# A fused attention and MLP kernel: quarters of M computed beside halves of the scores

## The chip, the cores and the metric

The kernel runs on one core of a Trainium2 chip. What counts is the device time of one execution in microseconds (us); of several runs the median is taken. TensorE (PE, with its weight loads as PEld) does the matrix products, VectorE (DVE) and ScalarE (ACT) read their results from the accumulation banks (PSUM) and do the rest, and SyncE (SP) issues all transfers (DMA).

## The reference

Eight batches of eight heads, 576 positions, head width 64. A packed set of 32 queries `p` attends to `k`, `v`; then every query attends to the 32 packed rows; the result goes through two feed-forward layers.

```python
def sm_attn(qq, kk, vv):
    s = scale * np.matmul(qq, kk.transpose(0, 1, 3, 2))
    a = np.exp(s - np.max(s, axis=-1, keepdims=True))
    return np.matmul(a / (np.sum(a, axis=-1, keepdims=True) + 1e-09), vv)
p_packed = sm_attn(p, k, v)
out = sm_attn(q, p_packed, p_packed)
x = out.transpose(0, 2, 1, 3).reshape(B * S, H * D)     # 4608 x 512
h = np.maximum(x @ w_in, 0.0); x = h * h @ w_out        # 512 -> 2048 -> 512
h = x @ w_in2; return (h / (1.0 + np.exp(-1.702 * h))) @ w_out2
```

## The kernel before

The program has two parts. The first, some 740 us long, does the attention and the first feed-forward layer, and prepares the weights of the second one beside it. The second part does the second layer; the change doesn't touch it.

**Slots.** The first layer runs in slots `(b, hf, fc)`: one batch, one half (288 positions), one of 16 chunks of 128 hidden units; from batch 2 on a batch is 32 slots in a row. Instead of `a @ v` and then `@ w_in`, the kernel multiplies the packed rows into the weights once for a batch: M = packed rows x `w_in`, made in four quarters `f` of 512 hidden units. A slot has a first product `h` (`mm1`, six matmuls of the attention `a` with M), the square of its positive part split into a high and a low number (`gh`; by `r`, `gf` and `gsplit`), and a second product `y` (`mm2`, twelve matmuls of `gh` with `w_out` into four banks `acc0` to `acc3`). The first product runs three slots ahead (`LA = 3`). At the end of a half (`fc` 15) the four banks are read out, by ACT (`ysb`) or, where a stored part is added, by DVE (`yp`), and slot `fc` 0 starts new sums in them.

**Attention beside it.** While batch b-1 goes through its 32 slots (from s0), the attention of batch b is spread over the same slots by a table: scores of the packed queries `s1` in two halves (slots 0 and 1), exponentials `s1b`, transposes `tr`, packed rows `pv` and `t2`, scores of all queries `s2a` in two halves (slots 12 and 17), `s2b`, `s2c`, and the quarters of M (`m_step`, slots 19, 21, 26, 29). In the traces both kinds of scores are called `s` and a quarter of M `m`. Each of them is one call of `heads`: eight small products that use a 64-row by 32-column part of the array each. They show as 16 matmuls, two rounds over the eight parts.

**Banks.** Of the eight banks, four are `acc`, two `mm` (used in turn by `h`) and two `at`: from batch 1 on all of the attention's products go to the `at` pair. A first half of `s1` is read twice: DVE takes the maxima (`L319`), then ACT copies it to `e` (`L323`). The second half stays in its banks until the exponentials. `s2a` is read by two DVE transposes (`L401`).

**Loads.** Tables also place the loads: `p` and all of `k` at slot -5, `v` at -2, `q` at 2, 3, 5, 6, and the eight halves of `w_in` (`win`, three buffers) at 9 and at the slots of the quarters of M.

The loop that sets the order:

```python
for s in range(done("y"), len(slots)):
    ...                              # gh of the slots up to s + 2
    drain(first, nfirst)             # h of slot s + 3
    drain(second, s)                 # y of slot s
    interleave(plan[s])              # the attention's steps of this slot
```

Of the kernel before, what the change touches and what calls it, by code (L numbers as in the profile page):

```python
# [75 lines left out]
def fused_kernel(ctx, tc, qT, kT, vv, pT, w_in, w_out, w_in2, w_out2, out):  # L76
# [216 lines left out]

    def att_tile(b, alt, name):

        pool, tag = (mm_p, "mm") if b == 0 and alt else (at_p, "at")
        return pool.tile([P, 512], F32, tag=tag, name=name)

    def heads(ps, w, x):

        n = None
        for hp in range(4):
            for r in range(2):
                rows = slice(64 * r, 64 * r + 64)
                xx = x(hp)[rows]
                n = xx.shape[-1]
                nc.tensor.matmul(ps[r][32 * hp:32 * hp + 32, :n], w(hp)[rows], xx, start=True, stop=True)  # L307

    def s1(b, hf):
        c = slice(hf * HS, (hf + 1) * HS)  # L310
        ps = [att_tile(b, hf, f"s1_{b}_{hf}_{r}") for r in range(2)]
        heads(ps, lambda hp: pt[b][:, hp, :], lambda hp: kt[b, hp][:, c])
        if hf == 0:
            rs[b] = st_p.tile([P, 6, 2], F32, tag="st", name=f"st{b}")
        st = rs[b]
        e1[b, "ps", hf] = ps
# [30 lines left out]
    def tr(b, r):  # L347
        e = e1.pop((b, r))
        if b == 0 and r == 1:
            t = y_p.tile([P, NDM * HS], F32, tag="y", name=f"e1t_{b}_{r}")[:, :5 * P]  # L350
        else:
            t = e1t_p.tile([P, 5 * P], F32, tag="e1t", name=f"e1t_{b}_{r}")
        t = e1T[b, r] = t.rearrange("p (c k) -> p c k", c=5)
        pa_ = att_tile(b, r, f"tr_{b}_{r}_a")
        pb_ = att_tile(b, r, f"tr_{b}_{r}_b")
        for c in range(4):
            nc.tensor.transpose(pa_[:, c * P:(c + 1) * P], e[:, c * P:(c + 1) * P], ident)  # L357
        nc.tensor.transpose(pb_[:64, :P], e[:, 512:576], ident)
        yield 1
        ta_ = t[:, 0:4, :].rearrange("p c k -> p (c k)")  # L360
        if b == 0:
            nc.vector.tensor_copy(ta_, pa_)
            yield 1
            nc.scalar.activation(t[:64, 4, :], pb_[:64, :P], AF.Copy)
        else:
            nc.scalar.activation(ta_, pa_, AF.Copy)
            yield 1
            nc.vector.tensor_copy(t[:64, 4, :], pb_[:64, :P])

    def pv(b, r):  # L370
        t = e1T.pop((b, r))
        v = vt.pop((b, r))
        ps = att_tile(b, r, f"pv_{b}_{r}")
# [69 lines left out]
    def s2c(b, hf):  # L443
# [3 lines left out]
        yield  # L447
        nc.vector.tensor_tensor(out=a[:, :, 1, :], in0=x, in1=a[:, :, 0, :].bitcast(F32), op=ALU.subtract)

    def m_step(b, f):  # L450
        w = [wt.pop((b, f, g)) for g in range(2)]
        if (b, f) == (0, 0):
            ps = [acc_p.tile([P, 512], F32, tag=f"acc{r}", name=f"m_{b}_{f}_{r}") for r in range(2)]
        else:
            ps = [at_p.tile([P, 512], F32, tag="at", name=f"m_{b}_{f}_{r}") for r in range(2)]
        heads(ps, lambda hp: ppT[b][:, 32 * hp:32 * hp + 32], lambda hp: w[hp // 2][:, hp % 2, :])
        yield 1
# [314 lines left out]
    def at(s, f, *a):  # L772
        plan[s].append((f, a))
# [83 lines left out]
    def token(k):  # L857
# [2 lines left out]
        g = running[k] if k in running and name != "warm" else macros[name](*map(int, a))  # L860
        running[k] = None if g is None or next(g, running) is running else g

    for b in range(1, B):
        if b == 1:
            s0 = 0
            at(43, m_step, 1, 2)
            at(47, m_step, 1, 3)
            for n, s in enumerate((40, 40, 43, 43)):
                at(s, load_win, 1, 2 + n // 2, n % 2)
            continue  # L870
        else:
            s0 = (b - 1) * 2 * NFC
            at_k, at_v, at_q, at_w = -5, -2, (2, 3, 5, 6), 9
            steps = [(0, s1, 0), (1, s1, 1), (4, s1b), (7, tr, 0), (8, pv, 0), (8, tr, 1), (9, pv, 1),
                     (10, t2), (12, s2a, 0), (16, s2b, 0), (17, s2c, 0), (17, s2a, 1), (20, s2b, 1), (26, s2c, 1)]

            steps += [(s, m_step, f) for f, s in enumerate((19, 21, 26, 29))]
        ld = loads(b)
        for n, (f, *a) in enumerate(ld):
            at(s0 + (at_k if n < 5 else at_v if n < 7 else at_q[n - 7]), f, *a)  # L880
        if b > 1:
            for s, f, *a in steps:
                at(s0 + s, f, b, *a)
        ws = [s for s, f, *_ in steps if f is m_step]
        if b == 2:
            at_w = 14
        for n in range(8):
            f = n // 2
            at(s0 + (at_w if n < 3 else ws[(n - 3) // 2]), load_win, b, f, n % 2)

# [106 lines left out]
    nfirst, nsplit = done("f"), done("g")  # L997
    for _ in range(4):
        ahead()
    for s in range(done("y"), len(slots)):  # L1000
        while nsplit < min(s + LA, nfirst):
            drain(parts, nsplit)
            nsplit += 1
        while nfirst < min(s + LA + 1, len(slots)):
            drain(first, nfirst)
            nfirst += 1
        while nsplit <= s:
            drain(parts, nsplit)
            nsplit += 1
        drain(second, s)  # L1010
        interleave(plan[s])
# [31 lines left out]
```

## Time and profile before

| | |
|---|---|
| three timed runs | median 1437.19 us, 1436.12 to 1437.35 |
| the profiled execution | 1436.79 us |
| its span, first to last instruction | 1434.9 us |
| PE busy, share of the span | 98% |
| PEld / DVE / ACT | 88% / 66% / 58% |
| granted TensorE clock, mean | 0.999 of full speed |

The profiled execution lies 0.4 us below the median. A busy PE isn't PE at its peak: matmuls overlap, so what a step costs is read from the start of one group to the start of the next.

### The profile page before, as it was taken

What the parts mean: (1) busy time and instruction counts of PE and PEld (TensorE: products, weight loads), DVE (VectorE), ACT (ScalarE), POOL (GpSimd) and SP (SyncE); (2) the same over time, 40 slices, a digit from 0 to 9 for tenths busy, and PEclk for the clock granted to TensorE, in tenths of its full rate; (3) what the DMA queues carried; (4) which work ended last, traced back from release to release, by engine and by line L of the source; (5) the groups of instructions that cost most, each with busy time, mean ns of one, the idle gap of its engine ahead of it and who ended that gap; (6) DMA issues with size and microseconds to landing.
All of it is one profiled execution on the core that took longest, in us unless ns stands there. A gap on an engine that the chain in (4) does not pass through costs nothing.

```text
span 1434.9 us, 24896 instructions
## 1 busy us (share of the span) xinstructions
PE 1412.7 (98%) x9734; PEld 1262.1 (88%) x9734; DVE 951.2 (66%) x1623; ACT 835.8 (58%) x1740; POOL 0.7 (0%) x6
## 2 busy tenths in 40 slices
PE   6999999999999999999999999999999999999999
PEld 4688989889898998999998888888888888999998
DVE  6896475756757657573255778577855875677585
ACT  5878676676776677765564544454444534544452
POOL 0000000000000000000000000000000000000000
PEclk9999999999999999999999999999999999999999
DMA  9848467576664756541325566656665676688675
GB/s 327 288 148 307 162 207 227 176 235 212 200 229 176 251 182 221 186 149 33 125 99 206 205 244 221 217 206 227 227 227 205 220 250 229 248 300 286 253 293 180
DMA packets 110934, 307.95 MB, mean 215 GB/s; under 512 B 9056, under 2 KB 52192, under 8 KB 96736
## 3 DMA queue, kind: packets, MB, share of 16 engines
q1 hardware_dynamic: 110816, 306.35, 62.1%
q8 instruction: 77, 1.26, 0.4%
q14 instruction: 41, 0.34, 0.1%
HBM read 250.94 MB, written 55.38 MB: 213 GB/s over the span
## 4 chain that ended last, share of the span: by engine, by line
PE 93%; DMA 3%; ACT 3%; DVE 1%; issue 0%; SPq 0%; DVEq 0%; ACTq 0%
PE h L112 37%; PE y L524 27%; PE o L112 24%; PE m L307 2%; PE s L307 1%; PE pv L377 1%; DMA wA<-w_d 1%; PE tr_a L357 1%; DMA win<-win_d 0%; DMA raw_wo<-in_w_out 0%; PE h L486 0%; DMA w_d<-wc 0%; DMA p<-in_pT 0%; PE warm L830 0%; ACT e L338 0%; ACT gh L202 0%
## 5 line engine op out<-in xcount | busy, mean ns | idle before, releaser
L524 PE MATMUL y<-gh,wo 128*128 128x288 f32 x2976 | 434.2, 295 | 0.4 <-ACT gh L202 0.2
L524 PEld LDWEIGHTS y<-gh,wo 128*128 128x128 f32 x2976 | 406.2, 188 | 4.4 <-ACT gh L202 1.3
L112 PE MATMUL h<-y,wA 128*128 128x512 f32 (+1 forms) x1680 | 349.8, 367 | 1.4 <-DMA wA<-w_d 1.4
L112 PE MATMUL o<-g,wB 128*128 128x512 f32 (+1 forms) x1680 | 349.0, 367 | 0.0
L112 PEld LDWEIGHTS h<-y,wA 128*128 128x128 f32 x1680 | 305.6, 188 | 42.1 <-issue 2.0
L112 PEld LDWEIGHTS o<-g,wB 128*128 128x128 f32 x1680 | 305.6, 188 | 39.6 <-DMA wB<-w_d 0.4
L112 PE MATMUL h<-a,M 128*128 128x288 f32 x1488 | 242.8, 299 | 1.3 <-ACT r L493 1.3
L112 PEld LDWEIGHTS h<-a,M 128*128 128x128 f32 x1488 | 207.7, 188 | 37.0 <-issue 27.7
L636 ACT ACTIVATE g<-hid 128x1024 fp32r<-128x1024 f32 (+1 forms) x140 | 132.8, 971 | 131.9 <-DVE hid L631 102.3
L204 DVE TENSOR_TENSOR gh<-gf,gh 128x288 fp32r<-128x288 f32 x248 | 111.6, 452 | 121.4 <-ACT gh L202 121.1
L612 DVE TENSOR_TENSOR g<-hid,g 128x1024 fp32r<-128x1024 f32 (+1 forms) x140 | 152.6, 1113 | 42.3 <-ACT g L636 40.7
L493 ACT ACTIVATE r<-h 128x288 f32<-128x288 f32 x256 | 104.1, 407 | 84.2 <-PE h L112 81.0
L700 ACT ACTIVATE r<-h 128x512 f32<-128x512 f32 (+1 forms) x120 | 66.6, 555 | 118.3 <-PE h L112 116.1
L708 DVE TENSOR_TENSOR hid<-h,r 128x512 f32<-128x512 f32 (+1 forms) x120 | 76.0, 634 | 81.7 <-PE h L112 65.3
L202 ACT ACTIVATE gh<-gf 128x288 fp32r<-128x288 f32 x248 | 108.6, 438 | 5.2 <-DVE gf L501 2.7
L718 DVE TENSOR_TENSOR hid<-hid,sg 128x512 f32<-128x512 f32 (+1 forms) x120 | 75.7, 631 | 47.1 <-ACT sg L714 47.0
L503 ACT ACTIVATE gf<-r 128x288 f32<-128x288 f32 x212 | 94.3, 445 | 6.6
L714 ACT ACTIVATE sg<-hid 128x512 f32<-128x512 f32 (+1 forms) x120 | 70.2, 585 | 30.5 <-DVE hid L708 30.3
L470 DVE TENSOR_TENSOR M<-m,M 128x512 fp32r<-128x512 f32 x62 | 41.9, 688 | 45.9 <-ACT M L468 45.2
L631 DVE TENSOR_TENSOR hid<-hid 128x1024 f32<-128x1024 f32 (+1 forms) x60 | 66.1, 1111 | 0.0
L468 ACT ACTIVATE M<-m 128x512 fp32r<-128x512 f32 x62 | 36.0, 593 | 39.8 <-PE m L307 39.7
L714 ACT ACTIVATE sg<-h 128x512 f32<-128x512 f32 (+1 forms) x40 | 22.3, 557 | 32.7 <-PE h L112 32.7
(110 smaller groups left out, 974.5 us busy)
## 6 DMA issues: line engine op xcount, KB each, us to landing
wB<-w_d SPq DMA_DIRECT2D x70, 1024.0 KB, 5.0
wA<-w_d SPq DMA_DIRECT2D x40, 1024.0 KB, 4.9
wA<-w_d SPq DMA_DIRECT2D x40, 768.0 KB, 6.2
win<-win_d SPq DMA_DIRECT2D x56, 512.0 KB, 5.1
w_d<-wc SPq DMA_DIRECT2D x112, 256.0 KB, 3.4
k<-in_kT SPq DMA_DIRECT2D x32, 288.0 KB, 5.4
y_d<-ysb SPq DMA_DIRECT2D x16, 576.0 KB, 3.8
v<-in_vv SPq DMA_DIRECT2D x16, 512.0 KB, 7.0
```

Of the source, the lines that this page charges most:

```text
L112: nc.tensor.matmul(ps, w, x, start=start and i == 0, stop=stop and i == n - 1, skip_group_check=more)
L202: nc.scalar.activation(hi, x, AF.Copy)
L204: nc.vector.tensor_tensor(out=lo, in0=x, in1=hi.bitcast(F32), op=ALU.subtract)
L493: nc.scalar.activation(r, ps[:, :HS], AF.Relu)
L503: nc.scalar.activation(g, r, AF.Square)
L524: nc.tensor.matmul(accs[d][:, :HS], w[:, d * P:(d + 1) * P], t[:, x_, :], start=first, stop=fc == seg[1] and d not in {o[0] for o in ops[n ...
L612: nc.vector.tensor_tensor(out=t[:, :, 1, :n], in0=src, in1=t[:, :, 0, :n].bitcast(F32), op=ALU.subtract)
L636: nc.scalar.activation(t[:, :, 0, :PAIRS[p]], gop[p, i, g, "src"], AF.Copy)
L700: nc.scalar.activation(t[:, 0, :n], bank[p, c, "1"][:, :n], AF.Copy)
L708: nc.vector.tensor_tensor(out=hid(p, c, blk), in0=bank[p, c, b][:, :n], in1=part[p, c, r][:, 0, :n], op=ALU.add)
L714: nc.scalar.activation(t, bank[p, c, "1"][:, :n] if blk == 2 else hid(p, c, blk), AF.Sigmoid, scale=GELU)
L718: nc.vector.tensor_tensor(out=hid(p, c, blk), in0=bank[p, c, "1"][:, :n] if blk == 2 else hid(p, c, blk), in1=part.pop((p, c, "sg", blk)), ...
```

## The change

From batch 3 on, each half of `s1` is issued together with a quarter of M of the batch before (quarters 2 and 3, at slots 0 and 4), and from batch 2 on each half of `s2a` with a quarter of its own batch (0 and 1, now at slots 17 and 22). The scores of such a pair go to the two `mm` banks, the quarter to the two `at` banks. In such a slot the order is: `y` of the slot, scores, quarter of M, the reading of the scores, and only then `h` of slot s + 3. The slot behind it issues its `y` ahead of its own `h`. Both halves of `s1` are now copied to `e`. Quarters 2 and 3 of the last batch stay alone.

```diff
 def att_tile(b, alt, name):
-    pool, tag = (mm_p, "mm") if b == 0 and alt else (at_p, "at")
+    pool, tag = (mm_p, "mm") if alt else (at_p, "at")
...
 def s1(b, hf):
-    ps = [att_tile(b, hf, f"s1_{b}_{hf}_{r}") for r in range(2)]
+    ps = [att_tile(b, b > 2 or b == 0 and hf, f"s1_{b}_{hf}_{r}") for r in range(2)]
...
-            if b > 0 and hf == 0:
+            if b > 2 or b > 0 and hf == 0:
...
 def s2a(b, hf):
-    ps = [att_tile(b, hf == 0, f"s2_{b}_{hf}_{r}") for r in range(2)]
+    ps = [att_tile(b, b > 1 or b == 0 and hf == 0, f"s2_{b}_{hf}_{r}") for r in range(2)]
...
+            slot_p, slot_k, slot_v, slot_q, slot_w = -11, (-11, -8, -6, -4), (-16, -14), (2, 5, 7, 9), (10, 12, 14)
...
+            joint[s0] = (s1, b, 0), (m_mm, b - 1, 2)
+            joint[s0 + 4] = (s1, b, 1), (m_mm, b - 1, 3)
+            at(s0 + 1, m_ev, b - 1, 2)
+            at(s0 + 5, m_ev, b - 1, 3)
+        joint[s0 + 17] = (s2a, b, 0), (m_mm, b, 0)
+        joint[s0 + 22] = (s2a, b, 1), (m_mm, b, 1)
...
+        slot_w += (18, 20, 23, 25, 33)
...
+        if s in joint:
+            lead_split(s, min(s + LA, nfirst))
+            drain(second, s)
+            (f, *a), (f2, *a2) = joint[s]
+            g = f(*a)
+            next(g)
+            drain(f2, *a2)
+            for _ in range(4 if f is s1 else 2):
+                next(g)
+            lead(s)
+            interleave([(lambda g=g: g, ())] + plan[s])
+        else:
+            if s - 1 not in joint:
+                lead(s)
+            drain(second, s)
+            lead(s)
+            interleave(plan[s])
```

`m_mm` is the matmul part of `m_step` and `m_ev` its reading, now apart; `lead(s)` issues `h` of slot s + 3 and `gh` of slot s.

The first place is PE at the change from batch 2 to batch 3 (slot 96, where the scores of batch 4 are due). `y_1_*` are the second products of the half that ends, `y_0_*` of the half that begins, `h_0_3` is a first product. Before:

```order
L524 MATMUL y_1_2_0_3695<-gh_1_15_4192,wo_1843 128x288
L524 MATMUL y_1_3_0_3698<-gh_1_15_4192,wo_1843 128x288
L112 MATMUL h_0_3_4306<-a_0_3738,M_0_3834 128x288 x6
L524 MATMUL y_0_0_0_4317<-gh_0_0_4237,wo_514 128x288 x2
L524 MATMUL y_0_1_0_4320<-gh_0_0_4237,wo_514 128x288 x2
L524 MATMUL y_0_2_0_4323<-gh_0_0_4237,wo_514 128x288 x2
L524 MATMUL y_0_3_0_4326<-gh_0_0_4237,wo_514 128x288 x2
```

After the change, at the same place:

```order
L538 MATMUL y_1_2_0_3681<-gh_1_15_4183,wo_1843 128x288
L538 MATMUL y_1_3_0_3684<-gh_1_15_4183,wo_1843 128x288
L538 MATMUL y_0_0_0_4276<-gh_0_0_4213,wo_514 128x288 x2
L538 MATMUL y_0_1_0_4279<-gh_0_0_4213,wo_514 128x288 x2
L538 MATMUL y_0_2_0_4282<-gh_0_0_4213,wo_514 128x288 x2
L538 MATMUL y_0_3_0_4285<-gh_0_0_4213,wo_514 128x288 x2
```

`h_0_3` no longer stands between the last matmuls of one half and the first of the next, which write the same four banks.

The second place is PE a little further on, behind these second products. `s_4_0_*` are the scores of batch 4 (two tiles), `m_2_*` is quarter 2 of M of batch 3, `h_0_3` and `h_0_4` are first products. Before:

```order
L307 MATMUL s_4_0_0_4333<-k_3_4156,p_4148 32x288
L307 MATMUL s_4_0_1_4334<-k_3_4156,p_4148 32x288
L112 MATMUL h_0_4_4353<-a_0_3738,M_1_3920 128x288 x6
L524 MATMUL y_0_0_0_4317<-gh_0_1_4271,wo_514 128x288 x2
L524 MATMUL y_0_1_0_4320<-gh_0_1_4271,wo_514 128x288 x2
```

After the change:

```order
L307 MATMUL s_4_0_0_4292<-k_3_4177,p_3894 32x288
L307 MATMUL s_4_0_1_4293<-k_3_4177,p_3894 32x288
L307 MATMUL m_2_0_4303<-win_2_0_3860,ppT_3558 32x512
L307 MATMUL m_2_1_4304<-win_2_0_3860,ppT_3558 32x512
L307 MATMUL m_2_0_4303<-win_2_0_3860,ppT_3558 32x512
L307 MATMUL m_2_1_4304<-win_2_0_3860,ppT_3558 32x512
L307 MATMUL m_2_0_4303<-win_2_1_3994,ppT_3558 32x512
L307 MATMUL m_2_1_4304<-win_2_1_3994,ppT_3558 32x512
L307 MATMUL m_2_0_4303<-win_2_1_3994,ppT_3558 32x512
L307 MATMUL m_2_1_4304<-win_2_1_3994,ppT_3558 32x512
L112 MATMUL h_0_3_4319<-a_0_3892,M_0_3783 128x288 x6
L538 MATMUL y_0_0_0_4276<-gh_0_1_4241,wo_514 128x288 x2
```

The eight products of the quarter of M follow the scores, and the next first product, `h_0_3`, comes behind both.

The third place is ACT in the same slot. `ysb` is the last of the four readings of `acc`, `e_4_0` and `e_4_1` are the copies of the scores, `r` the positive part of a first product. Before:

```order
L538 ACTIVATE ysb_1_4297<-y_1_3_0_3698 128x288
L202 ACTIVATE gh_0_2_4303<-gf_0_2_4283 128x288
L493 ACTIVATE r_0_3_4313<-h_0_3_4306 128x288
L323 ACTIVATE e_4_0_4345<-s_4_0_0_4333 128x288
L323 ACTIVATE e_4_1_4348<-s_4_0_1_4334 128x288
L202 ACTIVATE gh_0_3_4350<-gf_0_3_4315 128x288
```

After the change:

```order
L552 ACTIVATE ysb_1_4267<-y_1_3_0_3684 128x288
L202 ACTIVATE gh_0_2_4273<-gf_0_2_4253 128x288
L325 ACTIVATE e_4_0_4314<-s_4_0_0_4292 128x288
L325 ACTIVATE e_4_1_4317<-s_4_0_1_4293 128x288
L507 ACTIVATE r_0_3_4326<-h_0_3_4319 128x288
L202 ACTIVATE gh_0_3_4342<-gf_0_3_4328 128x288
```

The copies now stand ahead of `r_0_3`, since `h_0_3` now comes behind the scores.

## Rows read from the trace of the kernel before

**Rows 1.** The page's chain of work that ended last, by engine

```profile
PE 93%; DMA 3%; ACT 3%; DVE 1%; issue 0%; SPq 0%; DVEq 0%; ACTq 0%
```

**Rows 2.** Busy time by stretch, each one batch long: stretch, length, engines, clock, DMA

```profile
227.36:317.10 89.74, 88.44 (x797) 80.26 (x796) 57.17 (x131) 61.32 (x158) 0.00 (x0) 1.00 0.66 204
317.10:404.62 87.52, 87.52 (x797) 80.10 (x796) 58.96 (x137) 62.67 (x159) 0.00 (x0) 1.00 0.65 212
404.62:492.43 87.81, 87.81 (x797) 80.28 (x796) 58.84 (x134) 62.21 (x160) 0.00 (x0) 1.00 0.60 198
```

**Rows 3.** Timeline of PE, 270 to 345 us: start, length, line, instruction, count

```profile
308.76 1.09 PE L307 MATMUL m<-win,ppT 64*32 64x512 f32 x16
309.78 1.06 PE L112 MATMUL h<-a,M 128*128 128x288 f32 x6
...
313.05 1.75 PE L524 MATMUL y<-gh,wo 128*128 128x288 f32 x12
314.64 0.95 PE L112 MATMUL h<-a,M 128*128 128x288 f32 x6
315.42 1.74 PE L524 MATMUL y<-gh,wo 128*128 128x288 f32 x12
317.10 0.72 PE L307 MATMUL s<-k,p 64*32 64x288 f32 x16
317.74 1.06 PE L112 MATMUL h<-a,M 128*128 128x288 f32 x6
318.64 1.74 PE L524 MATMUL y<-gh,wo 128*128 128x288 f32 x12
```

**Rows 4.** Timeline of PE, instants in batch 0's two score groups

```profile
19.15 0.48 PE L307 MATMUL s<-q,ppT 64*32 64x288 f32 x8 [0.30 <-ACT ppT L389]
...
19.41 0.65 PE L307 MATMUL s<-q,ppT 64*32 64x288 f32 x9
...
19.66 0.44 PE L307 MATMUL s<-q,ppT 64*32 64x288 f32 x6
```

**Rows 5.** Timeline of all engines, 312.8 to 319.5 us

```profile
312.71 0.69 DVE L470 TENSOR_TENSOR M<-m,M 128x512 fp32r<-128x512 f32 x1 [1.44 <-ACT M L468]
...
314.46 1.30 ACT L538 ACTIVATE ysb<-y 128x288 f32<-128x288 f32 x4
...
317.93 0.82 DVE L319 TENSOR_REDUCE st<-s 128x1 f32<-128x288 f32 x2 [0.97 <-PE s L307]
318.42 0.78 ACT L323 ACTIVATE e<-s 128x288 f32<-128x288 f32 x2 [2.02 <-DVE st L319]
```

**Rows 6.** Line 323: durations in ns, least, median, most

```profile
L323 ACT ACTIVATE e<-s x14: 392/412/446, 46.2 to 581.6; 128x288 f32<-128x288 f32 x14
```

**Rows 7.** Timeline of all engines, 132.5 to 137.5 us

```profile
133.70 1.29 DVE L470 TENSOR_TENSOR M<-m,M 128x512 fp32r<-128x512 f32 x2 [2.11 <-ACT M L468]
134.45 0.13 PEld L307 LDWEIGHTS s<-k,p 64*32 64x32 f32 x2 [1.02 <-DVE M L470]
```

**Rows 8.** Timeline of all engines, 437.9 to 439.3 us

```profile
438.00 0.72 PE L307 MATMUL s<-q,ppT 64*32 64x288 f32 x16
...
438.84 0.48 DVE L401 STREAM_TRANSPOSE s2t<-s 128x288 f32<-128x288 f32 x1 [1.53 <-PE s L307]
```

**Rows 9.** Timeline of all engines, 222.5 to 229.5 us

```profile
224.77 1.54 DVE L536 TENSOR_TENSOR yp<-y,yp 128x288 f32<-128x288 f32 x4
...
227.36 0.72 PE L307 MATMUL s<-k,p 64*32 64x288 f32 x16
```

**Rows 10.** Timeline of PE, 100 to 112 us

```profile
108.85 1.77 PE L112 MATMUL h<-a,M 128*128 128x288 f32 x12
```

**Rows 11.** Timeline of PE, 283 to 289 us

```profile
285.01 1.06 PE L307 MATMUL m<-win,ppT 64*32 64x512 f32 x8
287.38 1.06 PE L307 MATMUL m<-win,ppT 64*32 64x512 f32 x8 [1.30 <-DMA win<-win_d]
```

**Rows 12.** The tile win: time of its transfers from issue to landing

```profile
DMA to landing us min/median/max: 2.9/5.5/8.7
```

More of the change, by code (lines that the diff above doesn't have):

```diff
@@ L319, in s1 @@
             nc.vector.tensor_reduce(out=st[:, hf, r:r + 1], in_=ps[r][:, :HS], axis=AX.X, op=ALU.max)
-            if b > 0 and hf == 0:
+            if b > 2 or b > 0 and hf == 0:
                 yield 1
-                e = e1[b, r] = e1_p.tile([P, S], F32, tag="e1", name=f"e1_{b}_{r}")
-                nc.scalar.activation(e[:, :HS], ps[r][:, :HS], AF.Copy)
+                if hf == 0:
+                    e1[b, r] = e1_p.tile([P, S], F32, tag="e1", name=f"e1_{b}_{r}")
+                e = e1[b, r][:, c]
+                nc.scalar.activation(e, ps[r][:, :HS], AF.Copy)
                 e1[b, "ps", hf][r] = e
@@ L353, in tr @@
         t = e1T[b, r] = t.rearrange("p (c k) -> p c k", c=5)
-        pa_ = att_tile(b, r, f"tr_{b}_{r}_a")
-        pb_ = att_tile(b, r, f"tr_{b}_{r}_b")
+        pa_ = att_tile(b, b == 0 and r, f"tr_{b}_{r}_a")
+        pb_ = att_tile(b, b == 0 and r, f"tr_{b}_{r}_b")
         for c in range(4):
@@ L372, in pv @@
         v = vt.pop((b, r))
-        ps = att_tile(b, r, f"pv_{b}_{r}")
+        ps = att_tile(b, b == 0 and r, f"pv_{b}_{r}")
         for c in range(5):
@@ L448, in s2c, with m_mm @@
         nc.vector.tensor_tensor(out=a[:, :, 1, :], in0=x, in1=a[:, :, 0, :].bitcast(F32), op=ALU.subtract)
+    mps = {}
     def m_step(b, f):
+        yield from m_mm(b, f)
+        yield 1
+        yield from m_ev(b, f)
+    def m_mm(b, f):
         w = [wt.pop((b, f, g)) for g in range(2)]
@@ L455, in m_step, with m_ev @@
             ps = [at_p.tile([P, 512], F32, tag="at", name=f"m_{b}_{f}_{r}") for r in range(2)]
+        mps[b, f] = ps
         heads(ps, lambda hp: ppT[b][:, 32 * hp:32 * hp + 32], lambda hp: w[hp // 2][:, hp % 2, :])
-        yield 1
+        return
+        yield
+    def m_ev(b, f):
+        ps = mps.pop((b, f))
         if b == 0 and 4 * f < NFULL:
@@ L861, in token @@
         running[k] = None if g is None or next(g, running) is running else g
+    joint = {}
     for b in range(1, B):
         if b == 1:
-            s0 = 0
             at(43, m_step, 1, 2)
@@ L870, in fused_kernel @@
             continue
-        else:
[L872 to L889, printed above, removed]
+        s0 = (b - 1) * 2 * NFC
+        if b == 2:
+            slot_p, slot_k, slot_v, slot_q, slot_w = -5, (-5, -5, -5, -5), (-2, -2), (2, 3, 5, 6), (14, 14, 14)
+            steps = [(0, s1, 0), (1, s1, 1), (4, s1b), (7, tr, 0), (8, pv, 0), (8, tr, 1), (9, pv, 1), (10, t2)]
+        else:
+            slot_p, slot_k, slot_v, slot_q, slot_w = -11, (-11, -8, -6, -4), (-16, -14), (2, 5, 7, 9), (10, 12, 14)
+            steps = [(6, s1b), (9, tr, 0), (10, pv, 0), (10, tr, 1), (11, pv, 1), (12, t2)]
+            joint[s0] = (s1, b, 0), (m_mm, b - 1, 2)
[4 more added lines that the diff above has]
+        joint[s0 + 22] = (s2a, b, 1), (m_mm, b, 1)
+        steps += [(18, m_ev, 0), (19, s2b, 0), (21, s2c, 0), (23, m_ev, 1), (25, s2b, 1), (27, s2c, 1)]
+        slot_w += (18, 20, 23, 25, 33)
+        if b == B - 1:
+            steps += [(26, m_step, 2), (29, m_step, 3)]
+            slot_w = slot_w[:-1] + (27,)
+        for t, f, *a in ((slot_p, load_p), *((slot_k[i], load_k, i) for i in range(4)), *((slot_v[i], load_v, i) for i in range(2)),
+                         *((slot_q[i], load_q, i) for i in range(4)), *steps,
+                         *((t, load_win, n // 2, n % 2) for n, t in enumerate(slot_w))):
+            at(s0 + t, f, b, *a)
     calm = [s for s in range(45, SB - 2 * NFC) if s % 16 in CALM]
@@ L999, in fused_kernel, with lead_split, lead @@
         ahead()
-    for s in range(done("y"), len(slots)):
-        while nsplit < min(s + LA, nfirst):
+    def lead_split(s, end):
+        nonlocal nsplit
+        while nsplit < end:
             drain(parts, nsplit)
             nsplit += 1
+    def lead(s):
+        nonlocal nfirst
+        lead_split(s, min(s + LA, nfirst))
         while nfirst < min(s + LA + 1, len(slots)):
@@ L1006, in fused_kernel @@
             nfirst += 1
[L1007 to L1011, printed above, removed]
+        lead_split(s, s + 1)
+    for s in range(done("y"), len(slots)):
+        if s in joint:
+            lead_split(s, min(s + LA, nfirst))
+            drain(second, s)
[13 more added lines that the diff above has]
+            interleave(plan[s])
         for _ in range(plan_end[s]):
```

## The prediction

> **What bounds the kernel now.** I read the chain of work that ended last first: 93% of it is PE [rows 1], so only time that PE loses or gains counts. Then the busy time by stretch, one batch each. In the second stretch PE is busy from end to end (87.52 of 87.52 us) at a granted clock of 1.00; the stretches around it are 2.2 and 0.3 us longer with the same matmuls [rows 2]. So in this part PE waits for nearly nothing, and a step costs what it adds to PE's own row of groups. That is read from the timeline of PE, start to start [rows 3]. A plain slot is 1.59 us of `y` and 0.78 of `h`, 2.37 in all (313.05 to 314.64 to 315.42). A group of scores in between costs more than its own 0.64 us (317.10 to 317.74): the `y` ahead of it takes 1.68 instead of 1.59, the `h` behind it 0.90 instead of 0.78. So 0.09 on the way in, 0.12 on the way out. A quarter of M takes 1.02 us (308.76 to 309.78) and pays the same way in and out.
>
> **What a pair saves on PE.** The first saving is one way in and one way out: 0.21 us. The second is inside the groups. No pair of scores and M stands side by side before, but batch 0 has two groups of scores in a row [rows 4]: their first three rounds start at 19.15, 19.41 and 19.66, so the second group starts 0.25 us behind the last round of the first, as if it were the same group. A lone group takes 0.64, so 0.14 of it is a tail behind its second round, paid only where another kind of matmul follows. M's rounds are then (1.02 - 0.14)/2 = 0.44 us. A pair is 2 x 0.25 + 2 x 0.44 + 0.14 = 1.52 us in place of 0.64 + 1.02 = 1.66: 0.14 saved, 0.35 with the way in and out. Bounds for the inner part: nothing, if M has to wait for the tail of the scores, and 0.14; I take 0.14, since rows 4 are the same kind of neighbours.
>
> The row shows a price for each change between whole-array and 64-by-32 matmuls. The Trainium skill's page "TensorEngine Tiling (Array Packing)", Tiling Modes, Key Properties, says that changing the tiling mode drains TensorE, and changing only the tile does not; by that rule too a pair drains once instead of twice, and rows 3 and 4 agree. It gives no duration.
>
> There are 22 pairs: ten with `s1` (batches 3 to 7), twelve with `s2a` (batches 2 to 7). On the matmuls alone that is 22 x 0.35 = 7.7 us. Now what the new order adds.
>
> **The scores must be out of their banks before the next first product.** Before, scores lay in the `at` pair and `h` in the `mm` pair; `h` never waited for them. Now the scores take both `mm` banks, and `h` of slot s + 3 needs the first back at once. Count from the start T of the scores. With `s2a` the first DVE transpose starts 0.84 after T (438.84, scores at 438.00) and takes 0.48 [rows 8]; with 0.06 from an end to the waiting weight load (DVE's first reading of M ends at 133.70 + 0.69 = 134.39, the load starts at 134.45 [rows 5, 7]) the bank is back at T + 1.38, ahead of the end of M at T + 1.52. M hides it; 0.14 us is left over. With `s1` the bank is read twice, one after the other: maxima from T + 0.83 (317.93), and the copy, released by them, from T + 1.32 (318.42) [rows 5], for 0.41 [rows 6]. The bank is back at T + 1.79, and `h` starts 0.27 late. So an `s1` pair saves 0.08, an `s2a` pair 0.35: 10 x 0.08 + 12 x 0.35 = 5.0 us. Bounds for the 0.27: nothing, if copy and maxima could run together, and 0.27 more for each 0.27 by which DVE comes late; DVE sat idle for 0.97 before these maxima [rows 5], so I take 0.27.
>
> **At slot 0 of a batch `y` loses its cover.** In the first `s1` pair of a batch, `y` of `fc` 0 directly follows `y` of `fc` 15, and writes the four `acc` banks that ACT is only now reading out. Before, an `h` of 0.78 lay in between. ACT's four readings end at 314.46 + 1.30 = 315.76 [rows 5]. What comes behind the last reading is seen at the start of batch 2's slots, where `y` does wait: the readings, there by DVE, end at 224.77 + 1.54 = 226.31, and the next group starts at 227.36 [rows 9], 1.05 later. So here the scores would start at 315.76 + 1.05 = 316.81; without a wait at 314.64 + 1.68 = 316.32. That is 0.49 lost, in four of the five batches. In batch 3's case (the one of rows 9) the readings already bound the end, so moving `h` behind them loses its whole 0.78. Sum 4 x 0.5 + 0.8 = 2.8 us. Bounds: nothing, if ACT comes earlier for having one positive part less, and 5 x 0.78 = 3.9; I take 2.8, since the readings start when the last matmuls end, which the change does not move.
>
> **Loads.** The stretch that is 2.2 us longer has a quarter of M that stood between its two halves: 285.01 to 287.38, for `win` [rows 11]. That half was loaded two slots (4.7 us) ahead of its use, and such a transfer takes 5.5 us in the median and 8.7 at most [rows 12]. Now it is issued at slot 18 for slot 22, four slots or 9.5 us ahead, and the last half of a batch at slot 33 for 36. So I count the 2.2 and 0.3 us [rows 2] as gained: 2.5. Only in the last batch is a half still loaded two slots ahead (27 for 29); the six such loads of before cost 2.5 together, so 0.4 for this one. Bounds: gain of nothing, if other transfers come in its way, and 2.5. The loads of `k` and `v` are only moved to where SP has slots to spare; `k` still has four slots.
>
> **Small things.** Of two `h` in a row the second costs 1.77 - 0.95 = 0.82 us instead of 0.78 to 0.79 [rows 3, 10]: 22 x 0.03 = 0.7 us lost. The ten added copies are 4 us of ACT, which is busy for 62 of 88 us [rows 2]: hidden, unless they stand ahead of the positive part that the next slots wait for. `h` of slot s + 3 is now issued 1.6 us nearer to its `y`, with some 5 us left; between them lie four operations on ACT and DVE of the size of those in rows 6 and 8, 0.4 to 0.5 us each, about 2 in all.
>
> **Sum.** 5.0 + 2.5 - 2.8 - 0.4 - 0.7 = 3.6 us. The profiled execution took 1436.8, so 1433.2; it lies 0.4 below the median, so for a median 1433.6. About 0.2%, or 2.9 us, is what a measurement of this kernel can tell from no change; the line lies at 1434.3.
>
> **Rivals.**
> Readings that come late (the other side). The matmuls of a pair get shorter, the readings don't. If DVE has one more operation of 0.69 us [rows 5] in hand when the scores end, each `s1` pair loses 0.69 and each `s2a` pair 0.69 - 0.14 = 0.55: 10 x 0.69 + 12 x 0.55 = 13.5 us, and the time is 1447. It decides from a mean lateness of 0.24 us on, where the 3.6 are gone (10 x 0.24 + 12 x 0.10), and means slower by 0.2% from 0.37. For it: DVE and ACT are busy for two thirds of these stretches. Against it: DVE was idle for 0.97 and 1.53 us before the readings at 317.93 and 438.84 [rows 5, 8], and a new slot has two `y`, 3.2 us without a first product, for it to catch up. Chance 0.13, nearly all of it slower. The Trainium skill's tiling page (Performance Considerations, PSUM Bottleneck) warns of this: tiling speeds up TensorE, not the evacuation of PSUM, which may become the bottleneck. For `s1` the trace already bears it out, by the 0.27.
>
> The wait for `win` moves instead of going: the gain shrinks to 3.6 - 2.5 = 1.1, time 1435.7 for the execution, 1436.1 for a median. For it: transfers of up to 8.7 us, and loads now spread among the stores. Against it: three to four slots of lead. Chance 0.12.
>
> No saving inside a pair: M waits for the tail of the scores. For `s2a` pairs 0.14 less, for `s1` pairs nothing less until M ends at T + 1.66, still ahead of 1.79: 12 x 0.14 = 1.7 less, time 1435.3. Together with a wait at each slot 0 at its upper bound (1.1 more) 1436.4. Chance 0.09.
>
> Readings that don't hold: `h` waits for the maxima alone, or the `acc` banks are read out early enough: 2.7 or 2.8 more, time 1430.9. Against the first speaks that ACT's copy began with the end of the maxima each time. Chance 0.08.
>
> **How the numbers follow.** The forecast, 1433.6, has a chance of 0.58, with a range of its own from 1431.5 to 1435.5 by its bounds; 0.42 of that lies below 1434.3. Faster: 0.42 + 0.08 = 0.50. Same: 0.16 + 0.12 + 0.09 + 0.02 = 0.39. Slower: 0.11. The range from 1430.0 to 1437.0 takes in all but the late readings and the far end of the last rival.
>
> **What would show it.** In the changed profile: a pair from the start of the scores to the next `h` of 1.5 us with `s2a` and 1.8 with `s1`; at slot 0 a `y` of about 2.1 us ahead of the scores; no PE wait for `win` but perhaps in batch 7; stretches of a batch of about 87.3 us (87.5 less two times 0.35 and 0.08, plus 0.5 and four times 0.03). The prediction is wrong if `s2a` pairs take more than 1.6 us, if `y` waits for `gh` in the slots behind a pair, or if transfers hold PE elsewhere.

## The result and the profile after

The changed kernel takes 1443.94 us in the median of six runs (1443.05 to 1448.71), the kernel before 1437.27 in six runs on the same chip: the ratio is 1.0053, with a 95% interval from 1.0035 to 1.0070. It is slower by half a per cent, 6.7 us, where 3.6 us of gain were forecast, and it lies outside the range. The profiled execution of the changed kernel took 1446.28 us, span 1444.5, 2.3 above its median; its granted clock is 0.999 on the mean, as before.

First the busy time by stretch, one batch of slots each, the view that answers to [rows 2]: the stretch, its length, busy time of PE, PEld, DVE, ACT and POOL, granted clock, DMA share, GB/s. Then before's fourth stretch, which [rows 2] doesn't hold. The third fence has the page's chain of work by engine and answers to [rows 1].

```profile
222.60:317.12 94.52, 87.99 (x796) 80.97 (x795) 57.35 (x131) 61.40 (x160) 0.00 (x0) 1.00 0.60 193
317.12:408.33 91.21, 88.26 (x797) 82.32 (x796) 60.20 (x137) 62.08 (x161) 0.00 (x0) 0.98 0.64 203
408.33:498.31 89.98, 86.93 (x797) 80.76 (x796) 58.66 (x134) 62.68 (x162) 0.00 (x0) 1.00 0.65 209
498.31:586.58 88.27, 87.42 (x797) 80.81 (x796) 56.92 (x131) 61.41 (x160) 0.00 (x0) 1.00 0.60 201
```

```profile
492.43:579.92 87.49, 87.49 (x796) 80.21 (x795) 56.67 (x131) 60.76 (x158) 0.00 (x0) 1.00 0.65 219
```

```profile
PE 85%; ACT 6%; DVE 4%; DMA 4%; issue 1%; SPq 0%; DVEq 0%; ACTq 0%
```

Before, PE was busy from end to end in three of these four stretches; now it loses 6.5, 3.0, 3.0 and 0.9 us in them (length less PE's busy time), and the chain of work holds 6% of ACT and 4% of DVE in place of 3% and 1%. The four stretches, slots 64 to 191, take 586.58 - 222.60 = 363.98 us; before, the same 128 slots took 579.92 - 227.36 = 352.56. That is 11.4 us longer. The spans differ by 9.6: the changed kernel reaches slot 64 4.8 us earlier and takes 2.9 more behind slot 191. Some 2.5 of either are two quarters of M (1.02 + 0.21 each), which the change moves from slots 32 to 63 into slots 192 to 223. So the loss is in slots 64 to 191, and it is their sum that the experiments below are read by, beside the times.

What PE does in them, from its timeline (start, length, line, instruction, count, and in brackets how long PE was idle and on whom it waited), at one pair that goes as forecast, one that doesn't, a slot 0, and a second pair that doesn't:

```profile
272.20 0.72 PE L307 MATMUL s<-q,ppT 64*32 64x288 f32 x16
272.71 1.06 PE L307 MATMUL m<-win,ppT 64*32 64x512 f32 x16
273.71 1.05 PE L112 MATMUL h<-a,M 128*128 128x288 f32 x6
...
285.78 0.67 PE L307 MATMUL s<-q,ppT 64*32 64x288 f32 x2
289.54 0.47 PE L307 MATMUL s<-q,ppT 64*32 64x288 f32 x7 [3.09 <-ACT r L507]
...
292.15 1.06 PE L112 MATMUL h<-a,M 128*128 128x288 f32 x6 [1.03 <-DVE s2t L403]
...
313.15 1.74 PE L538 MATMUL y<-gh,wo 128*128 128x288 f32 x12
315.23 1.97 PE L538 MATMUL y<-gh,wo 128*128 128x288 f32 x12 [0.33 <-ACT ysb L552]
317.12 0.72 PE L307 MATMUL s<-k,p 64*32 64x288 f32 x16
317.63 1.06 PE L307 MATMUL m<-win,ppT 64*32 64x512 f32 x16
318.91 1.06 PE L112 MATMUL h<-a,M 128*128 128x288 f32 x6 [0.21 <-ACT e L325]
...
378.39 0.72 PE L307 MATMUL s<-q,ppT 64*32 64x288 f32 x16
378.90 1.06 PE L307 MATMUL m<-win,ppT 64*32 64x512 f32 x16
382.31 1.07 PE L112 MATMUL h<-a,M 128*128 128x288 f32 x6 [2.34 <-DVE s2t L403]
```

The pair at 272.20 (slot 17 of the stretch) takes 1.51 us from the scores to `h`, M starting 0.51 after the scores: the forecast said 1.52 and 0.50. The pair with `s1` at 317.12 takes 1.79, and `h` waits 0.21 for the copy `e`: forecast 1.79. At 313.15 to 317.12 two `y` in a row wait for the readings of `acc`. All of that was in the sum. What was not is the pair of slot 22, the second half of `s2a` with quarter 1: at 285.78 it takes 6.37 us to `h`, at 378.39 3.92.

The sums, from the chain of waits (who waits for whom: us, times, longest):

```profile
PE h L112 <- DVE s2t L403: 5.4, 4, 2.3
PE s L307 <- ACT r L507: 3.1, 1, 3.1
PE h L112 <- ACT e L325: 2.5, 10, 0.3
```

The third is the forecast's 0.27 for each of ten `s1` pairs. The first two are the new ones, and all five of their waits are in slot 22. From the start of `y` of slot 20 to the start of `y` of slot 27 PE takes 18.35 us in batch 2, where nothing waits, and 23.20, 22.31, 21.12 and 18.83 in the four stretches. So the pair of slot 22 and the groups next to it lose 4.9, 4.0, 2.8 and 0.5 us, 12.1 in all. Less this loss the last three stretches are 87.2, 87.2 and 87.8 us long, where 87.3 were forecast; the first is 89.7.

Why ACT and DVE come so late there, first at 285.78. ACT's timeline:

```profile
282.16 0.45 ACT L517 ACTIVATE gf<-r 128x288 f32<-128x288 f32 x1
288.44 0.42 ACT L241 ACTIVATE wc<-sum 128x256 fp32r<-128x256 f32 x1 [5.84 <-DMA w_d<-wc]
...
289.10 0.39 ACT L507 ACTIVATE r<-h 128x288 f32<-128x288 f32 x1
```

ACT prepares weights of the second layer (`wc`) in one of three buffers, and waits 5.84 us for a store (`w_d<-wc`) to land and free one. Behind it in ACT's own order stands the positive part `r` at 289.10, which empties the `mm` bank that the second tile of the scores goes to. The scores stop after their first two matmuls, and go on at 289.54. SP's queue ahead of that:

```profile
277.03 0.56 SPq L173 DMA_DIRECT2D raw_p<-in_w_in  x1
...
278.28 0.42 SPq L281 DMA_DIRECT2D v<-in_vv  x1
278.75 0.56 SPq L282 DMA_DIRECT2D v<-in_vv  x1
279.43 1.93 SPq L249 DMA_DIRECT2D w_d<-wc  x2
```

Two transfers of `v`, which the change moved here, stand ahead of the stores, and all of it, a load of `win` too, leaves together behind a load of weights (`raw_p`) that had waited; the stores here need 8.0 us (median from issue to landing of the three between 274 and 290 us).

At 378.39 no transfer is late. DVE alone is (its timeline; the lines left out are three more sums of weights):

```profile
378.30 0.69 DVE L155 SCALAR_TENSOR_TENSOR x_p<-raw_p,x_p 128x512 int32<-128x512 int32 x1
378.91 0.45 DVE L204 TENSOR_TENSOR gh<-gf,gh 128x288 fp32r<-128x288 f32 x1
379.27 0.42 DVE L230 TENSOR_TENSOR sum<-x_p,x_p 128x256 f32<-128x256 f32 x1
379.61 0.75 DVE L450 TENSOR_TENSOR a<-s2x,a 128x576 fp32r<-128x576 f32 x1
...
381.41 0.45 DVE L204 TENSOR_TENSOR gh<-gf,gh 128x288 fp32r<-128x288 f32 x1
381.77 0.84 DVE L403 STREAM_TRANSPOSE s2t<-s 128x288 f32<-128x288 f32 x2
```

DVE has next to no idle time here. Conversions, sums of weights and the low part of the attention rows stand ahead of the transposes, which start 3.38 us after the scores instead of the 0.84 of [rows 8].

That this lateness is not new, the trace of before shows at a place that the prediction did not read. Its timeline at 525.8 us:

```profile
525.84 0.72 PE L307 MATMUL s<-q,ppT 64*32 64x288 f32 x16
526.48 1.06 PE L112 MATMUL h<-a,M 128*128 128x288 f32 x6
...
527.80 0.42 ACT L241 ACTIVATE wc<-sum 128x256 fp32r<-128x256 f32 x1 [4.91 <-DMA w_d<-wc]
...
528.96 0.48 DVE L401 STREAM_TRANSPOSE s2t<-s 128x288 f32<-128x288 f32 x1
```

ACT waits 4.91 us for a store, and DVE's first transpose starts 3.12 us after the scores; PE loses next to nothing. The scores lie in the `at` banks, which nothing else takes until the second half of these scores 12.7 us later, and the next `h` is issued right behind them.

### The profile page after: what moved, and what is told of

It is laid out like the page before. It is cut to its first block, busy times and chain, and to the rows that moved or that the text cites. A ratio compares the mean times of both kernels' runs of the same rounds, so it can differ in the third digit from the quotient of the medians.

```text
span 1444.5 us, 24966 instructions
## 1 busy us (share of the span) xinstructions
PE 1408.1 (97%) x9734; PEld 1264.9 (88%) x9734; DVE 952.1 (66%) x1623; ACT 835.7 (58%) x1750; POOL 0.7 (0%) x6
## 4 chain that ended last, share of the span: by engine, by line
PE 85%; ACT 6%; DVE 4%; DMA 4%; issue 1%; SPq 0%; DVEq 0%; ACTq 0%
PE h L112 35%; PE o L112 24%; PE y L538 22%; PE s L307 1%; PE m L307 1%; DMA w_d<-wc 1%; DMA raw_wo<-in_w_out 1%; PE pv L379 1%; ACT e L340 1%; ACT r L507 1%; DVE gh L204 1%; ACT gf L517 1%; ACT M L482 1%; ACT gh L202 1%; DMA wB<-w_d 1%
## 5 line engine op out<-in xcount | busy, mean ns | idle before, releaser
L112 PE MATMUL h<-a,M 128*128 128x288 f32 x1488 | 238.3, 299 | 9.9 <-DVE s2t L403 5.4
```

The costliest lines, as they stand in the source:

```text
L112: nc.tensor.matmul(ps, w, x, start=start and i == 0, stop=stop and i == n - 1, skip_group_check=more)
```

## The experiments

Two theories stood against each other. **Late readings**: ACT and DVE were often late by some us before, but the order hid it; the new order puts the scores into the `mm` banks, right behind a first product and right ahead of the next, so that each pair puts their lateness on PE's path twice (the scores wait for ACT's `r`, the next `h` for DVE's readings). **Late stores**: the moved loads of `p`, `k`, `v` crowd SP's queue, the stores of prepared weights land late, and ACT is held; the order does no harm by itself. Times are medians; a ratio is to the kernel before on the same chip, with its 95% interval. The median of before in the three sets was 1436.48 (E1 to E4), 1436.64 (E5 to E8) and 1436.41 (E9 to E12).

**E1, the loads back** where the kernel before has them, all else as changed:

```diff
-slot_p, slot_k, slot_v = -11, (-11, -8, -6, -4), (-16, -14)
+slot_p, slot_k, slot_v = -5, (-5, -5, -5, -5), (-2, -2)
```

> The loads of p, k and v of batches 3 to 7 go back to their slots of before (-5, -5, -2); the order of the products stays as changed. Theory of late stores (the moved loads crowd the queue just when prepared weights are stored, so ACT waits for a buffer): ACT's wait of 5.8 us for a store ahead of batch 3's slot 22 goes, and the time falls by 3 to 5 us, to 1439 to 1441. Theory of late readings (the new order lets every lateness of ACT and DVE reach PE, whatever its cause): ACT's waits for stores stay at 15 to 20 us in total, as before the change, and the time stays within 1.5 us of 1443.9.

1454.80 us, ratio 1.0121 (1.0096 to 1.0145): far slower still, which neither theory gave. ACT's waits for stores are what they were before the change, 20.0 us in 10 waits with a longest of 4.7 (before: 21.5 in 15, longest 4.9; changed: 17.9 in 8, longest 5.8), and still slots 64 to 191 take 596.25 - 226.22 = 370.03 us. PE's timeline, and ACT's behind it:

```profile
313.63 1.75 PE L538 MATMUL y<-gh,wo 128*128 128x288 f32 x12
318.89 1.33 PE L538 MATMUL y<-gh,wo 128*128 128x288 f32 x4 [3.52 <-ACT ysb L552]
```

```profile
316.25 0.42 ACT L241 ACTIVATE wc<-sum 128x256 fp32r<-128x256 f32 x1 [4.73 <-DMA w_d<-wc]
```

A wait of ACT of the size that before had for free costs PE 3.5 us at a slot 0, where `y` follows `y` and wants the `acc` banks that ACT has not read. There are three such waits, at slot 0 of batches 3, 4 and 7, of 4.1, 3.5 and 3.1 us, and PE runs on at a lower granted clock behind each (0.50 from 318.89 to 324.00). Slot 22 of batch 3 does get better: it loses 1.2 us in place of 4.9. So the move of the loads causes that one wait, but on balance it isn't what made the changed kernel slower; in the new order the old places are the worse ones.

**E2, no second pair**: the second half of `s2a` alone at slot 22 and in the `at` banks, quarter 1 at slot 24 and two loads of `win` two slots and one slot later.

```diff
-        joint[s0 + 22] = (s2a, b, 1), (m_mm, b, 1)
-        steps += [..., (23, m_ev, 1), ...]
+        steps += [..., (22, s2a, 1), (24, m_step, 1), ...]
```

> The pair at slot 22 is undone (second half of s2a and quarter 1 of M apart, as before, quarter 1 at slot 24); the other 16 pairs stay. Theory of late readings: the long waits at slot 22 in batches 3, 4 and 5 (4.9, 2.4 and 1.9 us, and 2.5 us of what follows them) go, six savings of 0.35 us are given back: 1435 to 1438. Theory of late stores: the stores are as late as with the change, the wait moves to another slot: 1440 to 1444.

1445.15 us, 1.0057 (1.0036 to 1.0077): no gain, 7 us above what late readings gave and 1 above late stores. DVE's waits at slot 22 are gone, but ACT's waits for stores (22.3 us, longest 5.5) reach PE as `h` waiting for `r` (7.1 us in 9 waits, the two long ones at slots 22 and 30 of batch 3). Taking the pair away does not take the lateness away.

**E3, slot 21 free**: no weight preparation is planned into slot 21 of a stretch, ahead of that pair.

```diff
-    calm = [s for s in range(45, SB - 2 * NFC) if s % 16 in CALM]
+    calm = [s for s in range(45, SB - 2 * NFC) if s % 16 in CALM and s % 32 != 21]
```

> The preparation of weights leaves out slot 21 of each batch, just ahead of the pair at slot 22; all else as changed. Theory of late readings: DVE has 2.7 us less in hand when the scores of that pair end, so the waits of batches 4 and 5 for the transposes shrink from 2.4 and 1.9 us to under 0.5: 1438 to 1441. Theory of late stores: no effect, or only where the stores happen to move, 1442 to 1445.

1441.13 us, 1.0031 (1.0020 to 1.0041): 2.8 us faster than the changed kernel, 0.1 above what late readings gave and below what late stores did. Slots 64 to 191: 579.36 - 222.23 = 357.13. With less in hand at slot 22, ACT and DVE are less late there, but not everywhere: the loss in batch 3 is down from 4.9 us to 0.8 and in batch 5 from 2.8 to nothing, but 2.4 are left in batch 4, and batches 6 and 7 lose 0.9 and 1.6 (after the change 0.5 and nothing).

**E4, first product ahead**: in a pair's slot `h` of slot s + 3 is issued ahead of the scores again, as before the change; the slot behind keeps its `y` first.

```diff
         if s in joint:
-            lead_split(s, min(s + LA, nfirst))
+            lead(s)
             drain(second, s)
...
-            lead(s)
             interleave([(lambda g=g: g, ())] + plan[s])
```

> In the slot of a pair the first product of slot s + 3 goes back ahead of the second product, as before the change; the pair itself, its banks, the loads and the order of the slot behind it stay as changed. Theory of late readings: the next first product then stands a second product (1.6 us) behind the pair, so the 0.27 us of each s1 pair and most of the waits at slot 22 go, and the wait of 0.5 to 0.8 us at slot 0 goes too, since a first product covers the reading of the sums again: 1428 to 1432. Theory of late stores: ACT is late all the same, and the time stays above 1438.

1438.96 us, 1.0013 (1.0001 to 1.0025): 5.0 us faster than the changed kernel, but 7 above what late readings gave, and where late stores put it (above 1438). The waits for the copy `e`, for the transposes and for `acc` at slot 0 are gone from PE's list. Left are scores that wait for ACT's `r` at slot 22 (5.0 us in 4 waits): the first product now stands just ahead of them, and they need its banks.

**E5, V later**: the changed kernel, with the loads of V in slots without weight preparation.

```diff
-slot_v = (-16, -14)
+slot_v = (-1, 0)
```

> The changed kernel, with the two loads of V of batches 3 to 7 issued in slots -1 and 0 of their batch, where no prepared weights are stored. Late stores: the moved loads crowd the queue in front of the stores of prepared weights, ScalarE waits 5.8 us for a buffer of prepared weights in batch 3 and the pair of slot 22 loses 4.7 us there; with V out of the way that wait falls below 2 us and the time to 1439 to 1440.5, while the waits on VectorE in batches 4 and 5 (3.9 and 2.8 us) stay. Late readings: the loads are not the cause, only the slack is gone; some wait of ScalarE for a store still reaches TensorE and the time stays within 1.5 of 1443.9.

1443.44 us, 1.0054 (1.0035 to 1.0073): no gain in the median, as late readings said. In its profile the one wait behaves as late stores said: ACT's wait ahead of that pair is 1.96 us in place of 5.84, and PE loses 1.0 there instead of 4.9; slots 64 to 191 take 585.39 - 225.15 = 360.24. The loads of V cause that one wait, but not the loss of the kernel: its seven runs spread from 1440.59 to 1449.19.

**E6 is E4 with V's loads of E5. E7 is E6, and in a pair M is issued ahead of the scores,** which then ask for ACT's `r` 0.9 us later. **E8 is E7 with E3's free slot** (slot 21 of a batch, not of each half).

```diff
             (f, *a), (f2, *a2) = joint[s]
+            drain(f2, *a2)
             g = f(*a)
             next(g)
-            drain(f2, *a2)
```

> In a slot with a pair the next slot's first product stands ahead of the pair again (as in the run before it of that form, 1439.0 us), and V's loads in slots -1 and 0. Late stores: what that form had left in batch 3 (2.4 + 1.3 + 1.2 us of waits for ScalarE's relu behind a 5.5 us wait for a store) goes: 1433.5 to 1435. Late readings: 1438 to 1440, since the waits only move to other places.

> As the run before, and in a pair the quarter of M is issued ahead of the scores. The scores then ask for their bank 1.2 us later, so that the waits of scores for a relu's reading in slot 22 (0.75 us in batch 4, 1.5 us in batch 5) go as well: 1431.5 to 1433.5 by late readings. By late stores nothing is gained over the run before.

> As the run before, and slot 21 of each half without weight preparation, so that ScalarE and VectorE come to the pair of slot 22 with less in hand. Late readings: 1431 to 1433, the pairs' saving of 0.35 us each stands and no wait above 0.5 us is left at slot 22. Late stores: the same time as the run before.

E6 1436.24 us, 1.0001 (0.9987 to 1.0015); E7 1434.57, 0.9992 (0.9981 to 1.0004); E8 1428.12, 0.9947 (0.9931 to 0.9964). E6 lies between what the two theories gave, E7 is 1 us above late readings (the wait at slot 22 of the first stretch stays in both), and the 1.7 us between them are not told from no change. E8 beats late readings by 3, where late stores gave no gain over E7: the free slot is worth 6.4 us here. It is faster than both kernels: by 8.5 us than before, by 15.8 than the changed one. Its stretches, in the columns of the first fence, and the same pair of slot 22 that took 6.4 us:

```profile
225.64:311.95 86.31, 86.31 (x803) 80.62 (x795) 56.95 (x130) 60.75 (x159) 0.00 (x0) 1.00 0.66 209
311.95:400.95 89.00, 87.49 (x803) 80.86 (x795) 56.72 (x130) 60.85 (x159) 0.00 (x0) 1.00 0.62 202
400.95:487.69 86.74, 86.39 (x804) 80.67 (x796) 56.89 (x130) 60.90 (x159) 0.00 (x0) 1.00 0.62 209
487.69:573.79 86.10, 86.10 (x803) 80.64 (x795) 58.40 (x132) 61.29 (x160) 0.00 (x0) 1.00 0.64 212
```

```profile
285.35 1.09 PE L307 MATMUL m<-win,ppT 64*32 64x512 f32 x16
286.23 0.69 PE L307 MATMUL s<-q,ppT 64*32 64x288 f32 x16
286.85 1.85 PE L538 MATMUL y<-gh,wo 128*128 128x288 f32 x12
288.54 1.77 PE L112 MATMUL h<-a,M 128*128 128x288 f32 x12
```

The pair takes 1.50 us and nothing waits. In the undisturbed stretches PE is busy from end to end, in 86.1 to 86.3 us; 87.5 in [rows 2] less four times 0.35 is 86.1. That is the saving the prediction worked out, all of it. The other two stretches still hold waits, 1.5 and 0.4 us.

**E9 to E12** ask where E8's gain comes from. E9 is the kernel before with only the loads of the change; E10 the kernel before with E8's loads of `p`, `k`, `v`, `q` and its free slot 21 (`win`'s loads and the table of steps stay as before); E11 the changed kernel's order of issue with V later and slot 21 free; E12 is E8 with V's loads back at -16 and -14.

```diff
 # E9 and E10, in the kernel before: p, k, v, q of batches 3 to 7
-at(s0 + (at_k if n < 5 else at_v if n < 7 else at_q[n - 7]), f, *a)
+at(s0 + spread[n], f, *a)   # -11, -11, -8, -6, -4, then v, then 2, 5, 7, 9
```

> The kernel before, its order of work kept, with the loads of P, K, V and Q of batches 3 to 7 in the slots that the change gives them (-11, -11, -8, -6, -4, -16, -14, 2, 5, 7, 9). Late stores: these slots crowd the stores of prepared weights whatever the order, so it loses 2 to 5 us against before (1438.5 to 1441.5). Late readings: the order of before has the slack for them: within 1.5 of before, and ScalarE's waits for a store change by a few us without a wait of TensorE.

> The kernel before, its order of work kept, with what the fastest form so far (1428.1 us) has beside the pairs: V's loads in slots -1 and 0, the other loads spread as in the change, slot 21 free of weight preparation. If the 8.5 us that that form gains over before come from the pairs (late readings: the saving was there and hidden by waits), this is within 2 us of before. If they come from the loads and the freed slot, it is at 1428 to 1431.

> The changed kernel with V's loads in slots -1 and 0 and slot 21 free of weight preparation, its order of issue otherwise kept (pair ahead of the next slot's first product, scores ahead of M). Late readings: only the waits go that come from work in hand at slot 22; the readings that the pair puts on the path elsewhere stay (0.26 to 0.5 us a pair): 1436 to 1439. Late stores: both causes are gone, and it is as fast as the fastest form, 1428 to 1430.

> The fastest form (first product ahead of the pair, M ahead of the scores, slot 21 free) with V's loads back in the change's slots -16 and -14. Late stores: the 5.5 us wait of ScalarE for a store in batch 3 is back and reaches TensorE: 1431 to 1434. Late readings: with slot 21 free and the first product ahead there is slack enough for it: 1428 to 1430.

| | median us | ratio (95%) | slots 64 to 191, us |
|---|---|---|---|
| before | 1437.27 | | 579.92 - 227.36 = 352.56 |
| changed | 1443.94 | 1.0053 (1.0035 to 1.0070) | 586.58 - 222.60 = 363.98 |
| E9: old order, loads spread | 1439.21 | 1.0010 (0.9995 to 1.0025) | 582.30 - 226.45 = 355.85 |
| E10: old order, E8's loads, slot 21 free | 1440.35 | 1.0021 (1.0007 to 1.0035) | 584.30 - 231.40 = 352.90 |
| E11: new order, E8's loads, slot 21 free | 1438.65 | 1.0021 (1.0010 to 1.0032) | 577.04 - 222.18 = 354.86 |
| E12: E8 with V's loads as changed | 1432.77 | 0.9970 (0.9958 to 0.9982) | 575.36 - 223.60 = 351.76 |
| E8 | 1428.12 | 0.9947 (0.9931 to 0.9964) | 573.79 - 225.64 = 348.15 |

E10 has slots 64 to 191 at before's length, 0.3 us apart: E8's loads and free slot alone bring nothing to the old order, so E8's gain came with the pairs and the places that go with them. Those of `win`'s loads are part of it: PE waits 2.2 us for `win` in E10's profile and not at all in E8's. (E10's median is 3.9 us above before, more than either expectation allowed. In its profile that lies ahead of slot 64, which it reaches 4.0 us later than before's; more on that below. Where its other runs lose time isn't shown.) E9 is where late stores put it, but its interval takes in no change, and its profile has one wait for `win`, 2.6 us, as its largest in these slots. E11 to E8 is the order of issue alone, first product ahead of the pair and M ahead of the scores: 10.5 us, and E11 is where late readings put it. E12 to E8 is the place of V's loads alone: 4.7 us by the medians, 3.3 by the ratios, which is what late stores can claim, and E12 is where they put it. E12's profile has them at slot 22 of the second stretch: ACT waits 5.0 us for a store, the scores wait 1.9 in two waits for `r`, and the granted clock is 0.59 in the 3.7 us behind.

So neither theory holds alone. Late readings missed E2, E4 and E12, late stores missed E3, E5, E8 and E11, and E1 came out as neither said. The runs agree with both halves put together: stores and the preparation of weights make ACT and DVE late, and the order of issue decides whether PE waits for it. No run gives the scores other banks in the changed order, so what the banks do by themselves is not shown.

## Why the prediction was wrong

Its terms for the matmuls came out as worked out:

- **A pair on PE**, where nothing is late: 1.51 us for a forecast of 1.52 with `s2a`; with the first half of `s1` 1.79 for 1.79, with the second 1.87, as its maxima start 0.08 later; the waits for the copy are 2.5 us in ten pairs, forecast 2.7.
- **Slot 0**: the two `y` ahead of the scores take 3.75 to 3.97 us in four batches where 1.59 + 1.68 = 3.27 would do, forecast 0.49 over; 4.16 at the fifth, in batch 3, 0.9 over, forecast 0.8.
- **`win`**: no wait of PE for it is left, so what those waits had cost (2.5 us by the prediction) is gone, and the 0.4 feared in the last batch was not lost.
- **Two `h` in a row** cost 1.59 (321.39 to 322.98), less than feared.

The step that failed is the one on the banks: "M hides it; 0.14 us is left over." It took DVE's start, 0.84 us after the scores, from one row [rows 8], a first half of `s2a` ahead of which DVE had been idle for 1.53 us, and used it for all twelve `s2a` pairs. Six of them are the second half, at slot 22, where DVE and ACT also prepare weights. There the transposes start up to 5.84 us after the scores (0.83 in all five pairs of slot 17 of the batches 3 to 7; at slot 22 of the same batches 5.84, 3.38, 2.88, 1.21 and 0.81). The 0.14 itself was right: the four late pairs lose their lateness less 0.14, that is 4.86, 2.41, 1.91 and 0.25 us. These 9.4 are most of the 12.1; the rest are waits of the `y` ahead in two of them (0.9 and 0.2) and 1.5 of a lower clock behind one (last section). The prediction's own first sign of being wrong, `s2a` pairs of more than 1.6 us, came in four of twelve. The rival "Readings that come late" named the mechanism and its price, 13.5 us and 1447, but put the chance at 0.13, by two rows at places of the same kind, and counted a lateness of one operation of 0.69 us at every pair; it is none at most pairs and 2 to 5 us at a few. Over the 22 pairs that is a mean lateness of (5.00 + 2.54 + 2.04 + 0.37) / 22 = 0.45 us, above the 0.37 that the rival named as the point from which the kernel is slower. Forecast gain 3.6 and loss 12.1 make 8.5 slower; the profiled executions differ by 9.5 (1446.28 - 1436.79). The 1.0 between is not assigned to a place; two `h` that each wait 0.37 for ACT's `r` (slot 8 of batches 3 and 7) and a transpose that waits 1.2 (slot 10 of batch 3) are candidates.

By the Trainium skill's page "TensorEngine Tiling (Array Packing)", Performance Considerations, PSUM Bottleneck, tiling speeds up TensorE but not the evacuation of PSUM, which may become the limit. This case agrees in a narrower sense: ACT and DVE stay at two thirds of the time, and it is the moment of one evacuation, not its rate, that holds PE.

The second thing left out is ACT's wait for stores. "The loads of `k` and `v` are only moved to where SP has slots to spare" rested on no row. V's loads at -16 and -14 fall among the stores, and E12 against E8 puts 4.7 us on them in the median. Yet they are not the main cause of the loss: E1 has them away and is slower, and E5 has them away and is no faster, because in the changed order ACT's waits for stores come through wherever they fall.

What the experiments show, then: the saving of a pair is real and whole (E8), and the loss is the order of issue around it, which makes PE wait at once for whatever ACT and DVE have in hand (E4, E11 against E8). How much they have in hand counts too: slot 21 left free is worth 2.8 us in the changed order (E3) and 6.4 in the other (E7 against E8). That the lateness was there before the change is shown by before's row at 525.84 and by before's 21.5 us of ACT's waits for stores.

## What to carry to other kernels

When work is moved onto banks or buffers that the main stream also uses, list how late the reading engine was at each place that the move touches, not at one, and give the pair the worst of them: a lateness that cost nothing in spare banks was paid here in full, less 0.14 us, on shared ones. Keep one product of the main stream between a side product and the next user of its bank. Putting the longer side product first may help too, though its 1.7 us (E6 to E7) are not told from no change. The same twenty-two pairs lost 6.7 us in one order and gained 8.5 in the other, with one slot kept free and two loads moved. An in-order engine that waits for a store holds up everything behind it, so stores that free buffers should not queue behind loads that nobody needs yet.

## What the runs showed of the hardware

A wait of PE can cost more than its length. The windows of the changed kernel around the wait at 378.39, which is part of the 4.0 us above (columns as in the first fence; the clock is the last number but two), and one window of E4 right behind two waits at slot 22, of 2.4 and 1.3 us:

```profile
379.78:382.31 2.53, 0.19 (x9) 0.01 (x1) 2.50 (x7) 0.00 (x0) 0.00 (x0) 1.00 0.77 260
382.31:383.21 0.90, 0.90 (x6) 0.90 (x7) 0.87 (x2) 0.00 (x0) 0.00 (x0) 1.00 0.65 254
383.21:385.79 2.58, 2.58 (x15) 2.58 (x13) 2.01 (x6) 1.50 (x4) 0.00 (x0) 0.57 0.47 124
385.79:387.93 2.14, 2.14 (x13) 2.14 (x13) 0.31 (x1) 0.56 (x2) 0.00 (x0) 0.72 0.90 320
```

```profile
289.77:292.15 2.38, 2.38 (x30) 0.74 (x30) 1.23 (x4) 1.87 (x4) 0.00 (x0) 0.50 0.12 40
```

PE is idle for 2.3 us, works again for 0.9 at full clock, and then the granted clock falls to 0.57 and 0.72 for 4.7 us (means of its two levels, 1.2 and 2.4 GHz, over a stretch; in E4 it is 0.50 throughout). The `y` in it takes 2.58 and the two `h` 2.14 us, where 1.59 each will do elsewhere: 1.5 us more. It is not so behind every wait: after the 3.1 us wait at 285.78 the clock stays at 1.00. The Trainium skill's page "TensorE: Matmul & The Clock Gate", What's actually happening, says that the clock is granted by how busy TensorE has been; the fall behind the 2.3 us wait agrees, and which waits bring one no run here shows.

A lower clock also shows early in the program, where neither the change nor E10's edit does anything. From 60 to 100 us the granted clock is 1.00 in the profile of before and in that of the changed kernel, and 0.87 in E10's:

```profile
60.00:100.00 40.00, 36.73 (x335) 31.11 (x335) 32.38 (x67) 31.18 (x74) 0.00 (x0) 0.87 0.47 162
```

That is 0.13 x 40 = 5 us as an estimate, near the 4.0 by which E10 reaches slot 64 later; so a comparison of two versions by one profile each should be made over the stretches that the change touches.
